# Attention and two MoE layers in one program: softmax sums in four column strips, new ranks for the attention's order, a softplus brought forward, evictions split by bank

## The chip, the core and the metric

The kernel runs on one core of one Trainium2 chip. The metric is device time in microseconds (us), from a run of the whole program. TensorE (PE) does the matrix products, VectorE (DVE), ScalarE (ACT) and GpSimd (POOL) the elementwise work, and SyncE (SP) issues the DMAs. Each engine works through its own list of instructions in order.

## What is computed

Three stages follow one another, each on the result of the one before: an attention with a decaying bias, an MLP with a softplus, and a second MLP with an RMS norm and a SiLU gate.

```
# attention: 4 batches x 8 heads, 576 positions, head width 64
scores = scale * np.matmul(q, k.transpose(0, 1, 3, 2))
cum = np.cumsum(np.maximum(s, 0.0), axis=-1)
bias = -(cum[:, :, :, None] - cum[:, :, None, :])
scores = np.where(causal, -1000000000.0, scores + np.minimum(bias, 0.0))
attn = np.exp(scores - np.max(scores, axis=-1, keepdims=True))
attn = attn / (np.sum(attn, axis=-1, keepdims=True) + 1e-09)
x = np.matmul(attn, v)                       # 2304 tokens x 512
...
# first MLP, 512 -> 2048 -> 512
h = x @ w_in
g = np.maximum(h, 0.0) + np.log1p(np.exp(-np.abs(h)))
x = g @ w_out
...
# second MLP, 512 -> 1536 -> 512
xn = x / np.sqrt(np.mean(x * x, axis=-1, keepdims=True) + 1e-06) * rms_g
g = xn @ w_gate
y = (g * (1.0 / (1.0 + np.exp(-g))) * (xn @ w_val)) @ w_out
```

## The kernel before, in words

**Stages.** In the profile the attention takes the first 221 us or so, the first MLP the time to about 632 us, the second the rest. The MLPs split each fp32 operand in a high and a low part of the faster type fp32r and multiply three times (high by high, low by high, high by low).

**Attention.** 32 heads are worked in 16 pairs p = 0 to 15. For each pair a fixed set of operations is listed by `attention_ops`, each with an engine, a planned duration, and what it depends on. The names that matter here:

- QT0 and QT1: q and k are loaded by LD (L391) and transposed on PE (L409). LV loads v (L398, L401).
- RA to RD with KA and so on: scores with queries on the partitions (L462, mask L470), from which DVE takes the row maxima. MT turns these maxima (L493), and DM writes them by DMA into the operand aq (L502, L503), to which POOL first writes a masked copy (AQ, L431).
- Ra to Rd with Ka and so on: scores the other way round, less the maximum (L518, mask L528), exponentials on ACT (Ea0 and so on, L535).
- A1 to A3: POOL adds the exponentials e of key blocks to zs (L546). V0 and V1: PE multiplies them by v (L552), into PSUM bank "o" (columns 0 to 383) and bank "x1" (columns 384 to 575).
- Z0 and Z1: PE sums zs and two leftover pieces of e over the partitions by a product with a matrix of ones (also recorded at L552, since one helper issues both). Z0 takes bank "o" again, Z1 the free half of "x1". Each head's sums come out on 64 partitions, all of them alike.
- O0 to O2: ACT copies PSUM to xz (L590). ZD (L594) fetches the sums by DMA into 128x9, ZR takes the reciprocal on DVE (L598), RS (L601) writes it out, BC (L606) spreads it over 64 partitions, XM multiplies on POOL (L610), XW (L614) writes x out.
- CF, CA, CD, CP, CH, CL: float64 weights of the MLPs are fetched (L227) and converted on ACT, DVE (L245 to L249) and POOL (L261, L282, L290), one step after another beside the attention.
- XL and X0 to X3 load and split the first tile of x for the first MLP; H0 and H1 are its first two products.

**What sets the order.** `attention_order` takes the operations one by one: among those that could start earliest by the planned durations it takes the one with the smallest rank, which is base times OFF["PER"] plus the offset OFF[name] (base is the pair's number, CONV0 and CONVR place the conversion steps). A change of the array's shape on PE is planned at 0.13. What comes out is the order of every engine's list; on the chip only the order is left of it.

**First MLP.** A step is m1_h (L792 to L794, 12 products), m1_sp (two softplus activations, L813 and L814), m1_gl (a subtraction, L818) and m1_y (L830, 12 products). Steps 0 and 1 have their m1_h in the attention's list; the rest follows when that list is through.

**Second MLP.** A step is m2_g (seven products A, B, C, D, in the manner of Strassen, L979 to L981 each) and m2_out (L1071), which adds into six PSUM banks m = 0 to 5 over 12 steps f. After each of three groups of 12 steps m2_evac copies the six banks out (L1082 on ACT, L1084 on DVE), two copies of 256 columns each, during steps f = 0 and f = 1 of the next group.

Of the kernel before, what the change touches and what calls it, by code (L numbers as in the profile page):

```python
# [36 lines left out]
OFF = {  # L37
    "PER": 11.74,
    "LV": 0.87,
    "QT0": -47.43,  # L40
    "QH0": 1.18,
    "QL0": -13.62,
    "QT1": -21.47,
    "QH1": -48.49,
    "QL1": -58.02,
    "AQ": -27.76,
    "RA": 67.90,
    "KA": 24.26,
# [15 lines left out]
    "MH": 34.21,
    "DM": -11.64,
    "Ra": -68.46,
    "Ka": -51.86,
    "Rb": 63.32,
    "Kb": 59.10,
    "Rc": 112.60,  # L70
    "Kc": -29.92,
    "Rd": 123.04,
    "Kd": -71.46,
    "Ea0": 22.03,
    "Ea1": -44.32,
    "Eb0": -51.97,
    "Eb1": -36.15,
    "Ec0": -74.59,
    "Ec1": 59.54,
    "Ed0": 45.74,  # L80
    "Ed1": 67.75,
    "A1": -21.66,
    "A2": -50.66,
    "A3": 70.17,
    "V0": -16.24,
    "V1": 79.45,
    "Z0": -16.76,
    "Z1": 87.12,
    "O0": 136.78,
    "O1": -45.76,  # L90
# [24 lines left out]
    "X3": -59.99,
    "H0": -23.02,
    "H1": -64.43,
}
CONV0 = 7.439
CONVR = 1.0130  # L120
OFF2 = {
# [24 lines left out]
def attention_moe_kernel(ctx, tc, q, k, v, s, w_in, w_out, w_gate, w_val, w_out2, rms_g, out):  # L146
# [47 lines left out]
    def f32(ap):  # L194
        return ap.bitcast(F32)
# [381 lines left out]

    IS = 384

    def a_ox(p, part):  # L580
        if ("xz", p) not in st:
            st["xz", p] = pools["xo"].tile([P, 2, S], F32, tag="xz", name="xz", bufs=2)
        xz = st["xz", p]
        if part < 2:
            jobs = ((part, slice(0, IS), st.pop((("o", "oz")[part], p))[:, 0:IS]),)
        else:
            x = st.pop(("x1", p))
            jobs = ((0, slice(IS, S), x[:, 0:S - IS]), (1, slice(IS, S), x[:, S - IS:2 * (S - IS)]))
        for w, c, x in jobs:
            nc.scalar.activation(out=xz[:, w, c], in_=x, func=AF.Copy, bias=(0.0, 1e-9)[w])  # L590
# [26 lines left out]
    def attention_ops():  # L617
# [8 lines left out]
        op(("GL", 0), "POOL", 2.9, g_load, [], 1, lat=4.0)  # L626
        for n, du in enumerate((1.9, 1.4, 1.3, 1.3)):
            op((f"G{n}", 0), "DVE", du, lambda n=n: g_part(n), [(f"G{n - 1}" if n else "GL", 0)], 1)
        for p in range(NP):
# [40 lines left out]
            add("A1", "POOL", 2.2, lambda p=p: a_a(p, 0), es[:6] + old(2, "Z0", "Z1"))  # L670
# [15 lines left out]
        for c, (ph, ch) in enumerate(CONV):  # L686
# [19 lines left out]
        for a in range(KD):  # L706
            op((f"X{a}", 0), "DVE", 0.8, lambda a=a: x_split(0, a, nc.vector), [("XL", 0), ("QT1", NP - 1)] + [(f"X{a - 1}", 0)] * (a > 0), NP)
        for i in range(2):
            op((f"H{i}", 0), "PE", 2.1, lambda i=i: m1_h(i),
               [(f"X{a}", 0) for a in range(KD)] + [("MT", NP - 1), ("CL", NA - 1), ("CP", len(CONV) - 1)] + [("R" + x, p) for x in "abcd" for p in (NP - 2, NP - 1)], NP, mode="f")  # L710
        for o in ops:
# [97 lines left out]
    def m1_sp(i):  # L809
        h = st.pop(("h", i))  # L810
        l = st["l", i] = m1_tile("l", 2)
        gh = st["gh", i] = m1_tile("gh", 3, F32R)
        nc.scalar.activation(out=l, in_=h, func=AF.Softplus)  # L813
        nc.scalar.activation(out=gh, in_=h, func=AF.Softplus)  # L814

    def m1_gl(i):
        gl = st["gl", i] = m1_tile("gl", 3, F32R)
        nc.vector.tensor_tensor(out=gl, in0=st.pop(("l", i)), in1=f32(st["gh", i]), op=ALU.subtract)  # L818
# [173 lines left out]
    def m2_g(n, fill=None):  # L992
# [25 lines left out]
        if f == 1 and g > 0:  # L1018
            m2_evac(g - 1, 1)
        if n:  # L1020
# [19 lines left out]
        if fresh:  # L1040
            m2_evac(g - 1, 0)
        if n + 1 < NS2:
# [30 lines left out]

    def m2_evac(g, h):
        W = DM // 2
        for m in range(3 * h, 3 * h + 3):
            r = 2 * T * g + m * P
            for i, c in enumerate((slice(0, W), slice(W, DM))):
                ob = y_tile() if g < NG - 1 or m % 2 else m1_tile("gl", 3)
                ob, src = ob[:, 0:W], st["o2"][m][:, c]  # L1080
                if m % 2:
                    nc.scalar.activation(out=ob, in_=src, func=AF.Copy)  # L1082
                else:
                    nc.vector.tensor_copy(out=ob, in_=src)  # L1084
                nc.sync.dma_start(out=out[r:r + P, c], in_=ob)

    def m2_end():
# [4 lines left out]
        m2_out(n, 0)  # L1092
        m2_evac(NG - 1, 0)
        m2_out(n, 1)
        m2_evac(NG - 1, 1)


    with tc.manual_schedule():
# [22 lines left out]
        with ExitStack() as es0:  # L1121
# [113 lines left out]
```

## Time and profile before

| | |
|---|---|
| device time, median of 3 runs | 1061.88 us (1059.81, 1061.88, 1062.24) |
| the profiled execution's own time | 1059.71 us |
| its span from the first to the last instruction | 1057.9 us |
| PE busy | 1029.3 us (97% of the span) |
| DVE busy | 693.4 us (66%) |
| POOL busy | 570.0 us (54%) |
| ACT busy | 540.6 us (51%) |
| mean granted clock of PE | 0.998 |

The shares are means over the three stages. A row of a timeline gives the start, the duration (for several instructions in a row, from the first to the last end), the engine, the line, the operation with its output and inputs, their shapes and how many; in brackets stands how long the engine was idle before and what it waited for. Matmuls overlap: a row's duration is longer than the step to the next row.

### The profile page before, as it was taken

How to read it: one execution, taken by the hardware profiler on the slowest of the kernel's cores; microseconds unless marked ns; L12 is line 12 of the kernel's file. 1: busy time of each engine (PE TensorE's matmuls, PEld its weight loads, DVE VectorE, ACT ScalarE, POOL GpSimd, SP SyncE). 2: the span in 40 equal slices, each digit the busy share in tenths (PEclk: the TensorE clock that was granted, in tenths of full speed). 3: DMA queues.
4: the chain of work that ended last, by engine and by line, in shares of the span. 5: the costliest groups of instructions: out<-in, count | busy, mean ns of one | idle time of the engine just before them, and what ended most of it. 6: DMA issues, size and time to landing. Idle time of an engine off the chain costs nothing.

```text
span 1057.9 us, 19448 instructions
## 1 busy us (share of the span) xinstructions
PE 1029.3 (97%) x7212; PEld 953.8 (90%) x7212; DVE 693.4 (66%) x1141; ACT 540.6 (51%) x1189; POOL 570.0 (54%) x477
## 2 busy tenths in 40 slices
PE   6999999999999999999999999999989999899997
PEld 5788877889999999999989998999979999799997
DVE  8888988418776756889898654545664346734444
ACT  2455666536656544544544544445554445644443
POOL 4378878736766433555767245355453433644331
PEclk9999999999999999999999999999999999999999
DMA  8367664345555575766542323224242233333221
GB/s 155 78 161 172 166 164 134 106 133 159 173 154 161 184 257 179 231 230 194 146 151 84 117 81 98 70 86 161 88 130 71 81 121 104 99 100 89 86 70 60
DMA packets 143758, 139.68 MB, mean 132 GB/s; under 512 B 68656, under 2 KB 118960, under 8 KB 143664
## 3 DMA queue, kind: packets, MB, share of 16 engines
q1 hardware_dynamic: 143632, 138.44, 44.5%
q8 instruction: 57, 0.93, 0.4%
q14 instruction: 37, 0.30, 0.1%
q0 software_dynamic: 32, 0.00, 0.0%
HBM read 106.73 MB, written 31.53 MB: 131 GB/s over the span
## 4 chain that ended last, share of the span: by engine, by line
PE 60%; DVE 7%; issue 3%; POOL 3%; DMA 2%; ACT 2%; SPq 0%; POOLq 0%; ACTq 0%; DVEq 0%
PE y L830 12%; PE o L1071 10%; PE A L979 4%; PE A L981 4%; PE A L980 4%; PE D L981 3%; PE D L979 3%; PE D L980 3%; PE h L792 3%; PE h L794 3%; PE h L793 3%; PE x L1071 2%; PE x L792 1%; PE x L794 1%; PE x L793 1%
## 5 line engine op out<-in xcount | busy, mean ns | idle before, releaser
L925 POOL TENSOR_TENSOR w<-wl,w 128x512 fp32r<-128x512 f32 x108 | 140.1, 1313 | 211.7 <-ACT w L924 211.7
L1071 PE MATMUL o<-w,gg 128*128 128x512 f32 x540 | 153.3, 393 | 0.3
L830 PE MATMUL y<-gh,w 128*128 128x384 f32 x768 | 149.8, 335 | 2.9 <-ACT gh L814 1.7
L830 PEld LDWEIGHTS y<-gh,w 128*128 128x128 f32 x768 | 134.4, 188 | 4.5 <-ACT gh L814 2.0
L1071 PEld LDWEIGHTS o<-w,gg 128*128 128x128 f32 x540 | 100.8, 188 | 19.4 <-ACT yt L1082 0.9
L979 PE MATMUL A<-xf,w 128*128 128x384 f32 x288 | 97.2, 338 | 6.2 <-DVE l L1047 4.7
L980 PE MATMUL A<-xf,w 128*128 128x384 f32 x288 | 96.9, 336 | 0.7 <-DVE xf L970 0.7
L981 PE MATMUL A<-xf,w 128*128 128x384 f32 x288 | 97.0, 337 | 0.0
L1047 DVE TENSOR_TENSOR l<-A,gh 128x384 f32<-128x384 f32 x36 | 20.0, 556 | 115.8 <-ACT w L924 113.3
L535 ACT ACTIVATE e<-t 128x448 f32<-128x448 f32 (+2 forms) x128 | 56.4, 505 | 71.3 <-PE t L528 66.4
L818 DVE TENSOR_TENSOR gl<-l,gh 128x384 fp32r<-128x384 f32 x96 | 79.3, 831 | 16.1 <-ACT gh L814 16.0
L261 POOL TENSOR_TENSOR wf<-ur 128x512 int32<-128x512 int32 x44 | 62.6, 1424 | 50.4 <-DVE ur L249 36.2
L485 DVE TENSOR_REDUCE mc<-s 128x2 f32<-128x512 f32 (+4 forms) x160 | 76.3, 534 | 19.0 <-PE s L470 15.0
L792 PE MATMUL h<-xh,w 128*128 128x384 f32 x256 | 85.6, 335 | 0.0
L793 PE MATMUL h<-xl,w 128*128 128x384 f32 x256 | 85.5, 334 | 0.0
L794 PE MATMUL h<-xh,w 128*128 128x384 f32 x256 | 85.5, 334 | 0.0
L830 PE MATMUL y<-gl,w 128*128 128x384 f32 x384 | 82.4, 335 | 2.3 <-DVE gl L818 2.2
L245 DVE TENSOR_SCALAR ur<-ur 128x512 f32<-128x512 f32 x68 | 51.3, 754 | 35.2 <-ACT ur L238 35.2
L979 PE MATMUL D<-xf,w 128*128 128x384 f32 x216 | 72.9, 338 | 0.0
L981 PE MATMUL D<-xf,w 128*128 128x384 f32 x216 | 72.8, 337 | 0.0
L980 PE MATMUL D<-xf,w 128*128 128x384 f32 x216 | 72.5, 336 | 0.0
L261 POOL TENSOR_TENSOR w<-ur 128x512 int32<-128x512 int32 x24 | 34.8, 1451 | 68.7 <-DVE ur L249 48.1
(171 smaller groups left out, 2662.8 us busy)
## 6 DMA issues: line engine op xcount, KB each, us to landing
wl<-wf SPq DMA_DIRECT2D x108, 256.0 KB
raw<-in_moe_w_out_dram SPq DMA_DIRECT2D x28, 512.0 KB
wf<-w SPq DMA_DIRECT2D x24, 512.0 KB
raw<-in_moe_w_in_dram SPq DMA_DIRECT2D x16, 512.0 KB
raw<-in_moe_w_gate_dram SPq DMA_DIRECT2D x12, 512.0 KB
raw<-in_moe_w_val_dram SPq DMA_DIRECT2D x12, 512.0 KB
xr<-x SPq DMA_DIRECT2D x28, 192.0 KB
qn<-in_q_dram SPq DMA_DIRECT2D x16, 288.0 KB
```

What stands on the lines that cost most here:

```text
L261: nc.gpsimd.tensor_tensor(out=w.bitcast(I32), in0=u, in1=r3, op=ALU.add)
L485: nc.vector.reduce_max(out=o, in_=x, axis=AX.X, negate=True)
L792: nc.tensor.matmul(o, wh, xh, start=start, stop=False)
L793: nc.tensor.matmul(o, wh, xl, start=False, stop=False)
L794: nc.tensor.matmul(o, wl, xh, start=False, stop=stop)
L818: nc.vector.tensor_tensor(out=gl, in0=st.pop(("l", i)), in1=f32(st["gh", i]), op=ALU.subtract)
L830: nc.tensor.matmul(y[m][:, 0:T], x[:, m * P:(m + 1) * P], r, start=first and x is w[0] and r is gh, stop=last and r is gl)
L925: nc.gpsimd.tensor_tensor(out=t[:, 1, 0:w], in0=src, in1=f32(t[:, 0, 0:w]), op=ALU.subtract)
L979: nc.tensor.matmul(o, wh[:, c], xh, start=first, stop=False, skip_group_check=True)
L980: nc.tensor.matmul(o, wh[:, c], xl, start=False, stop=False, skip_group_check=True)
L981: nc.tensor.matmul(o, wl[:, c], xh, start=False, stop=last, skip_group_check=True)
L1071: nc.tensor.matmul(st["o2"][m], x[:, m * P:(m + 1) * P], r, start=(f == 0 and k == 0), stop=(f == F2 - 1 and k == 2))
```

## The change

1. **Sums.** Z0 and Z1 become one operation Z. The weights are 32 columns of ones instead of 64, and each of the two heads gets two strips of 32 output partitions: the strips par = 0 take 128 columns of e and 160 of zs, the strips par = 1 take 288 columns of zs and 64 of e. All sums go into the free part of bank x1; bank o holds products with v alone. O1 copies 288 columns of sums, O2 copies 192 columns of x once instead of two pieces, and ZD reads four partitions of 288 sums. Z has an array shape ("mode") of its own.
2. **Ranks.** Planned durations are raised (CD 2.8 to 4.4, CP 1.29 to 1.43, X 0.8 to 1.2 and smaller ones), and all offsets in OFF are new, so the order of the attention's lists is another one throughout.
3. **Softplus.** m1_sp and m1_gl of the first MLP's steps 0 and 1 go into the attention's list as SP0, SP1, SG0 and SG1, with tiles borrowed from the attention's pools.
4. **Evictions.** m2_evac takes a list of banks. For the first two groups even banks go to ACT and odd ones to DVE (before, the other way round), banks 0 and 2 at the old place in step f = 0, bank 1 after that step's second sigmoid, banks 3, 4 and 5 in step f = 1. The last group stays as it was.

```diff
 OFF = {
-    "PER": 11.74,
-    "LV": 0.87,
...
+    "PER": 14.93,
+    "LV": 83.11,
...
-CONV0 = 7.439
-CONVR = 1.0130
+CONV0 = 0.746
+CONVR = 1.0075
...
-    def a_z(p, part):
+    IS = 384
+    IZ = 288
+    IO = S - IS
+
+    def a_z(p):
         zs, e = st["zs", p], st["e", p]
-        one = f32(ones)[:, 0:D]
-        if part == 0:
-            o = st["oz", p] = ps_1("o0")
-            jobs = ((one, zs, 0, P, 256), (one, e, 0, 0, P))
-        else:
-            o = st["x1", p]
-            jobs = ((one, zs, 256, 192, 192), (low, e, 768, 320, 64))
-        a_pv([(lambda hd, lt=lt: lt, lambda hd, x=x, c=c, w=w: x[:, hd, c:c + w], oc, w, part == 0 and n == 0)
-              for n, (lt, x, c, oc, w) in enumerate(jobs)], o)
...
+        one = f32(ones)[:, 0:32]
+        o = st["x1", p]
+        for lt, par, x, c, oc, w in ((one, 1, zs, 160, 0, IZ), (one, 0, e, 0, 0, P),
+                                     (one, 0, zs, 0, P, IZ - P), (low[:, 0:32], 1, e, 768, 224, 64)):
+            for hd in range(2):
+                r = 64 * hd + 32 * par
+                nc.tensor.matmul(o[r:r + 32, IO + oc:IO + oc + w], lt, x[:, hd, c:c + w], start=False,
+                                 stop=x is e or par == 0, skip_group_check=True)
...
-        nc.sync.dma_start(out=z, in_=st["xz", p][0:D + 1:D, 1])
+        nc.sync.dma_start(out=z, in_=st["xz", p][0:P:32, 1, 0:IZ])
...
-            add("V1", "PE", 1.45, lambda p=p: a_v(p, 1), es + ["LV"], alloc=[("x", [("O2", p)])], mode="c")
-            add("Z0", "PE", 0.67, lambda p=p: a_z(p, 0), ["A3", "V0"], alloc=[("o", [("O1", p)])], mode="c")
-            add("Z1", "PE", 0.46, lambda p=p: a_z(p, 1), ["A3", "V1"], mode="c")
+            add("V1", "PE", 1.45, lambda p=p: a_v(p, 1), es + ["LV"], alloc=[("x", [("O1", p), ("O2", p)])], mode="c")
+            add("Z", "PE", 0.72, lambda p=p: a_z(p), ["A3", "V1"], mode="z")
...
-            cv("CD", "DVE", 2.8, w_conv_d, ["CA"])
-            cv("CP", "POOL", 1.29, w_conv_p, ["CD"] + ([("CL" if c - 3 < NA else "CS", c - 3)] if c > 2 else []))
+            cv("CD", "DVE", 4.4, w_conv_d, ["CA"])
+            cv("CP", "POOL", 1.43, w_conv_p, ["CD"] + ([("CL" if c - 3 < NA else "CS", c - 3)] if c > 2 else []))
...
+        for i in range(2):
+            op((f"SP{i}", 0), "ACT", 2.1 - 1.25 * i, lambda i=i: m1_sp(i), [(f"H{i}", 0)]
+               + [(f"E{x}{hd}", p) for x in "abcd" for hd in range(2) for p in (NP - 2, NP - 1)], NP)
+            op((f"SG{i}", 0), "DVE", 0.6, lambda i=i: m1_gl(i), [(f"SP{i}", 0)], NP)
...
         if f == 1 and g > 0:
-            m2_evac(g - 1, 1)
+            m2_evac(g - 1, (3, 4, 5))
...
         if fresh:
-            m2_evac(g - 1, 0)
+            m2_evac(g - 1, (0, 2))
...
         act(out=s1, in_=gB, func=AF.Sigmoid)
+        if fresh:
+            m2_evac(g - 1, (1,))
...
-                if m % 2:
+                if m % 2 == (g == NG - 1):
                     nc.scalar.activation(out=ob, in_=src, func=AF.Copy)
```

The order shows what the ranks do. PE in the middle of the attention, the sums of a pair before the change (zs, e, ones and low are the operands named above):

```order
L528 LDWEIGHTS mask_135
L528 MATMUL t<-ident_134,mask_135 128x64
L552 MATMUL o_3045<-zs,ones 64x256 x2
L552 MATMUL o_3045<-e,ones 64x128 x2
L552 MATMUL x_2859<-zs,ones 64x192 x2
L552 MATMUL x_2859<-e,low 64x64 x2
L493 MATMUL mT<-ident,mc_208 128x128
L409 MATMUL qkT<-ident,qn 128x96 x6
```

And the sums of a pair after it:

```order
L473 LDWEIGHTS mask_135
L473 MATMUL s<-ident_134,mask_135 128x64
L581 MATMUL x_3120<-zs,ones 32x288 x2
L581 MATMUL x_3120<-e,ones 32x128 x2
L581 MATMUL x_3120<-zs,ones 32x160 x2
L581 MATMUL x_3120<-e,low 32x64 x2
L465 MATMUL s<-all_146,aq 128x512 x2
L465 MATMUL s<-hl 128x512 x2
```

The sums had stood between Kd of one pair and MT with the transposes of a later one; now they stand between KA and RB of a later pair, and the products with v, which have the sums' old array shape, stand elsewhere. A pair has five changes of the array's shape on PE instead of four.

SP, which issues the DMAs, at the program's start, from the eighth row of its list on, before (qn, kn and vn are q, k and v; raw is a step of float64 weights; aq<-mt is DM of pair 0; ahead of these stand the q and k of two pairs and pair 0's first v):

```order
L401 DMA vn_212<-in_v_dram 64x2x64
L398 DMA vn_214<-in_v_dram 128x4x64 x2
L401 DMA vn_214<-in_v_dram 64x2x64
L323 DMA all_145<-in_s_dram 32x1x576 x2
L398 DMA vn_216<-in_v_dram 128x4x64 x2
L401 DMA vn_216<-in_v_dram 64x2x64
L391 DMA qn<-in_q_dram 96x12x64
L391 DMA kn<-in_k_dram 96x12x64
L391 DMA qn<-in_q_dram 96x12x64
L391 DMA kn<-in_k_dram 96x12x64
L227 DMA raw<-in_moe_w_in_dram 128x4x128
L502 DMA aq<-mt 2x4x128
```

And after, where the q and k of two pairs stand ahead and no v:

```order
L230 DMA raw<-in_moe_w_in_dram 128x4x128
L230 DMA raw<-in_moe_w_out_dram 128x512
L326 DMA all_145<-in_s_dram 32x1x576 x2
L394 DMA qn<-in_q_dram 96x12x64
L394 DMA kn<-in_k_dram 96x12x64
L394 DMA qn<-in_q_dram 96x12x64
L394 DMA kn<-in_k_dram 96x12x64
L394 DMA qn<-in_q_dram 96x12x64
L394 DMA kn<-in_k_dram 96x12x64
L401 DMA vn_212<-in_v_dram 128x4x64 x2
L404 DMA vn_212<-in_v_dram 64x2x64
L505 DMA aq<-mt 2x4x128
```

Two weight fetches, of which one stood later, come first now; the q and k of a fifth pair are added ahead of DM of pair 0, and the v of two pairs have gone behind it.

ACT at the end of the attention before (o_ and x_ are the banks o and x1, h the first MLP's products):

```order
L535 ACTIVATE e<-t 128x320 x2
L590 ACTIVATE xz<-o_4047 128x384
L590 ACTIVATE xz<-o_4072 128x384
L590 ACTIVATE xz<-x_4055 128x192 x2
L590 ACTIVATE xz<-o_4085 128x384
L590 ACTIVATE xz<-x_4094 128x192 x2
L590 ACTIVATE xz<-o_4111 128x384
L813 ACT_TABLE_LOAD
L813 ACTIVATE l<-h 128x384
L814 ACTIVATE gh<-h 128x384
```

And after:

```order
L538 ACTIVATE e<-t 128x320 x2
L821 ACT_TABLE_LOAD
L821 ACTIVATE l<-h 128x384
L822 ACTIVATE g<-h 128x384
L589 ACTIVATE xz<-o_4021 128x384
L589 ACTIVATE xz<-x_4005 128x192
L821 ACTIVATE l<-h 128x384
L822 ACTIVATE g<-h 128x384
L589 ACTIVATE xz<-x_4005 128x288
L589 ACTIVATE xz<-o_4060 128x384
```

The table load and the first pair of softplus activations, which had come after all of the attention's evictions, now follow the last exponentials directly; the evictions O0 to O2 of the last two pairs come after them, with the second softplus pair in between.

## Rows read from the trace of the kernel before

**Rows 1.** Windows view: PE, PEld, DVE, ACT, POOL busy us; PEclk, DMA share, GB/s

```profile
12.00:24.00 12.00, 11.87 (x101) 9.88 (x100) 10.38 (x25) 1.34 (x5) 2.93 (x5) 1.00 1.00 183
96.00:108.00 12.00, 12.00 (x175) 9.63 (x173) 10.19 (x20) 7.39 (x19) 10.07 (x8) 1.00 0.73 174
```

**Rows 2.** Timeline of PE, the sums of one pair; a mask product elsewhere

```profile
97.26 0.23 PE L528 MATMUL t<-ident,mask 64*128 64x64 bf16 x4
97.42 0.65 PE L552 MATMUL o<-zs,ones 128*64 128x256 f32 x4
97.90 0.39 PE L552 MATMUL o<-e,ones 128*64 128x128 f32 x4
98.12 0.50 PE L552 MATMUL x<-zs,ones 128*64 128x192 f32 x4
98.66 0.33 PE L493 MATMUL mT<-ident,mc 128*128 128x128 f32 x1
...
203.98 0.23 PE L528 MATMUL t<-ident,mask 64*128 64x64 bf16 x4
204.05 0.46 PE L518 MATMUL t<-aq,all 41*128 41x448 f32 x2
```

**Rows 3.** Waits of PE over the span: us in total, times, longest

```profile
PE A L979 <- DVE l L1047: 4.7, 2, 2.4
PE o L552 <- ACT xz L590: 0.7, 1, 0.7
```

**Rows 4.** Timeline of ACT and PE where the first MLP begins

```profile
221.42 1.28 ACT L813 ACT_TABLE_LOAD   x1
224.81 1.50 PE L830 MATMUL y<-gh,w 128*128 128x384 f32 x7 [1.66 <-ACT gh L814]
```

**Rows 5.** Timelines of DVE, POOL and PE at the second group's start

```profile
774.39 1.41 DVE L1084 COPY yt<-o 128x256 f32<-128x256 f32 x4
775.72 0.54 DVE L1047 TENSOR_TENSOR l<-A,gh 128x384 f32<-128x384 f32 x1
782.96 0.75 DVE L1084 COPY yt<-x 128x256 f32<-128x256 f32 x2
...
775.55 1.00 POOL L970 TENSOR_TENSOR xf<-sq,xf 128x384 fp32r<-128x384 f32 x1
...
776.41 0.41 PE L979 MATMUL A<-xf,w 128*128 128x384 f32 x1 [2.34 <-DVE l L1047]
777.18 0.33 PE L980 MATMUL A<-xf,w 128*128 128x384 f32 x1
783.05 0.49 PE L1071 MATMUL o<-w,gg 128*128 128x512 f32 x1
783.85 0.47 PE L1071 MATMUL x<-w,gg 128*128 128x512 f32 x1 [0.31 <-DVE yt L1084]
```

**Rows 6.** Timelines of SP's queue and PE in the first 40 us

```profile
18.93 1.56 SPq L227 DMA_DIRECT2D raw<-in_moe_w_in_dram  x1
24.66 0.62 SPq L502 DMA_DIRECT2D aq<-mt  x1
...
28.96 1.32 PE L518 MATMUL t<-hl 64*128 64x448 f32 x6
39.51 0.76 PE L518 MATMUL t<-hl 64*128 64x448 f32 x6
```

**Rows 7.** Timelines of SP's queue and POOL around a pair's sums

```profile
99.35 0.58 SPq L594 DMA_DIRECT2D z<-xz  x1
111.35 0.58 SPq L594 DMA_DIRECT2D z<-xz  x1
...
109.11 0.75 POOL L431 TENSOR_SCALAR aq<-all,oh 128x576 fp32r<-128x576 f32 x1 [1.04 <-PE t L518]
112.30 1.43 POOL L610 TENSOR_TENSOR xz<-xz,rb 128x576 f32<-128x576 f32 x1 [0.22 <-DMA rb<-rd]
116.91 1.00 POOL L546 TENSOR_TENSOR zs<-zs,e 128x384 f32<-128x384 f32 x1
```

More of the change, by code (lines that the diff above doesn't have):

```diff
@@ L64 @@
[L64 to L90, printed above, removed]
@@ L120 @@
-CONVR = 1.0130
+    "PER": 14.93,
+    "LV": 83.11,
+    "QT0": 5.81,
+    "QH0": -39.55,
+    "QL0": -143.55,
+    "QT1": -11.31,
+    "QH1": 21.73,
+    "QL1": 14.30,
+    "AQ": 47.79,
+    "RA": 60.80,
+    "KA": 40.06,
+    "RB": 64.05,
+    "KB": -14.02,
+    "RC": 47.61,
+    "KC": 7.02,
+    "RD": -116.26,
+    "MA0": -138.12,
+    "MA1": 54.17,
+    "MB0": -67.30,
+    "MB1": -72.90,
+    "MC0": 31.97,
+    "MC1": 39.81,
+    "MD0": 31.08,
+    "MD1": 36.24,
+    "MN": 58.58,
+    "MT": -4.50,
@@ new lines @@
+    "MH": 25.08,
+    "DM": -19.33,
+    "Ra": 14.80,
+    "Ka": -41.55,
+    "Rb": 56.23,
+    "Kb": 10.35,
+    "Rc": 87.09,
+    "Kc": -21.91,
+    "Rd": 94.14,
+    "Kd": -8.05,
+    "Ea0": 54.85,
+    "Ea1": 27.06,
+    "Eb0": -66.79,
+    "Eb1": 59.21,
+    "Ec0": 91.89,
+    "Ec1": 91.42,
+    "Ed0": -2.82,
+    "Ed1": 6.60,
+    "A1": -39.80,
+    "A2": -48.49,
+    "A3": -96.30,
+    "V0": 56.77,
+    "V1": 53.07,
+    "Z": 36.84,
+    "O0": -58.45,
+    "O1": -36.49,
+    "O2": 66.31,
@@ new lines @@
+    "ZD": 10.01,
+    "ZR": -50.07,
+    "RS": -45.48,
+    "BC": -11.58,
+    "XM": -56.10,
+    "XW": -55.44,
+    "LD": -68.54,
+    "CF": -33.75,
+    "CA": 98.32,
+    "CD": -20.13,
+    "GL": 54.71,
+    "G0": 71.14,
+    "G1": -4.52,
+    "G2": 6.70,
+    "G3": -50.59,
+    "CP": -61.13,
+    "CH": 54.18,
+    "CL": -20.47,
+    "CS": 31.87,
+    "XL": -29.93,
+    "X0": -48.73,
+    "X1": -45.79,
+    "X2": 65.94,
+    "X3": -5.03,
+    "H0": -34.45,
+    "H1": -109.57,
+    "SP0": -60.0,
@@ L121 @@
+    "SP1": -60.0,
+    "SG0": -60.0,
+    "SG1": -60.0,
+}
+CONV0 = 0.746
+CONVR = 1.0075
 OFF2 = {
@@ L583, in a_ox @@
         xz = st["xz", p]
[L584 to L590, printed above, removed]
+        w, c, src, x, n, b = ((0, 0, "o", 0, IS, 0.0), (1, 0, "x1", IO, IZ, 1e-9), (0, IS, "x1", 0, IO, 0.0))[part]
+        nc.scalar.activation(out=xz[:, w, c:c + n], in_=st[src, p][:, x:x + n], func=AF.Copy, bias=b)
     def a_zd(p):
         z = st["z", p] = pools["sml"].tile([P, 9], F32, tag="z", name="z", bufs=2)
-        nc.sync.dma_start(out=z, in_=st["xz", p][0:D + 1:D, 1])
+        nc.sync.dma_start(out=z, in_=st["xz", p][0:P:32, 1, 0:IZ])
     def a_zr(p):
@@ L626, in attention_ops @@
         op(("GL", 0), "POOL", 2.9, g_load, [], 1, lat=4.0)
-        for n, du in enumerate((1.9, 1.4, 1.3, 1.3)):
+        for n, du in enumerate((1.9, 1.4, 1.5, 2.5)):
             op((f"G{n}", 0), "DVE", du, lambda n=n: g_part(n), [(f"G{n - 1}" if n else "GL", 0)], 1)
@@ L669, in attention_ops @@
             es = [f"E{x}{hd}" for x in "abcd" for hd in range(2)]
-            add("A1", "POOL", 2.2, lambda p=p: a_a(p, 0), es[:6] + old(2, "Z0", "Z1"))
+            add("A1", "POOL", 2.2, lambda p=p: a_a(p, 0), es[:6] + old(2, "Z"))
             add("A2", "POOL", 1.6, lambda p=p: a_a(p, 1), ["A1", "Ed0", "Ed1"])
@@ L706, in attention_ops @@
         for a in range(KD):
-            op((f"X{a}", 0), "DVE", 0.8, lambda a=a: x_split(0, a, nc.vector), [("XL", 0), ("QT1", NP - 1)] + [(f"X{a - 1}", 0)] * (a > 0), NP)
+            op((f"X{a}", 0), "DVE", 1.2, lambda a=a: x_split(0, a, nc.vector), [("XL", 0), ("QT1", NP - 1)] + [(f"X{a - 1}", 0)] * (a > 0), NP)
         for i in range(2):
             op((f"H{i}", 0), "PE", 2.1, lambda i=i: m1_h(i),
-               [(f"X{a}", 0) for a in range(KD)] + [("MT", NP - 1), ("CL", NA - 1), ("CP", len(CONV) - 1)] + [("R" + x, p) for x in "abcd" for p in (NP - 2, NP - 1)], NP, mode="f")
+               [(f"X{a}", 0) for a in range(KD)] + [("MT", NP - 1), ("CL", NA - 1), ("CP", len(CONV) - 1)] + [("R" + x, p) for x in "abcd" for p in (NP - 2, NP - 1)] + [("H0", 0)] * i, NP, mode="f")
+        for i in range(2):
+            op((f"SP{i}", 0), "ACT", 2.1 - 1.25 * i, lambda i=i: m1_sp(i), [(f"H{i}", 0)]
+               + [(f"E{x}{hd}", p) for x in "abcd" for hd in range(2) for p in (NP - 2, NP - 1)], NP)
+            op((f"SG{i}", 0), "DVE", 0.6, lambda i=i: m1_gl(i), [(f"SP{i}", 0)], NP)
         for o in ops:
@@ L810, in m1_sp @@
         h = st.pop(("h", i))
-        l = st["l", i] = m1_tile("l", 2)
-        gh = st["gh", i] = m1_tile("gh", 3, F32R)
+        if i < 2:
+            if "l01" not in st:
+                st["l01"] = pools["e"].tile([P, 2, 1600], F32, tag="e", name="l")
+                st["g01"] = pools["split"].tile([P, 4, S], F32R, tag="hl", name="g", bufs=3)
+            l, gh = st["l", i], st["gh", i] = st["l01"][:, i, 0:T], st["g01"][:, i, 0:T]
+        else:
+            l = st["l", i] = m1_tile("l", 2)
+            gh = st["gh", i] = m1_tile("gh", 3, F32R)
         nc.scalar.activation(out=l, in_=h, func=AF.Softplus)
@@ L816, in m1_gl @@
     def m1_gl(i):
-        gl = st["gl", i] = m1_tile("gl", 3, F32R)
+        gl = st["gl", i] = m1_tile("gl", 3, F32R) if i > 1 else st["g01"][:, 2 + i, 0:T]
         nc.vector.tensor_tensor(out=gl, in0=st.pop(("l", i)), in1=f32(st["gh", i]), op=ALU.subtract)
@@ L1072, in m2_out, with m2_evac @@
                              stop=(f == F2 - 1 and k == 2))
-    def m2_evac(g, h):
+    def m2_evac(g, ms):
         W = DM // 2
-        for m in range(3 * h, 3 * h + 3):
+        for m in ms:
             r = 2 * T * g + m * P
```

65 lines of the change are left out of this document (7 added, 58 removed).

## The prediction, made before the changed kernel ran

> **What bounds the kernel now.** I read the busy shares first, then windows, then PE's waits, then the timelines where PE waits. In the attention's middle PE is busy for all 12.00 of 12.00 us, while DVE has 10.19 and POOL 10.07 [rows 1]. One pair's fetch of sums starts 12.00 us after the other's [rows 7], so a pair costs 12.0 us and PE sets it: what is taken from PE's list there is gained, so long as the other engines keep up. In the MLPs PE is nearly full too; its waits there are few, and this change touches those of rows 3, where VectorE's L1047 ends 4.7 us at two places and ScalarE's eviction one of .7. At the program's start it is different: DMA share 1.00 and DVE 10.38 of 12 us, and PE's rows are long there [rows 1, 6].
>
> **The sums on PE.** The block is read from the last mask product at 97.26 to MT at 98.66 [rows 2]. From the mask products to the first sum are .16; where the same four mask products are followed by a product of the shape that PE already has, .07 (203.98 to 204.05) [rows 2]. That leaves .09 for a change of shape. The sums run from 97.42 to 98.66, 1.24, with the change back. Both heads' 128 columns, each of which is passed twice as fp32, take 97.90 to 98.12, .22, so .86 ns for a column and pass, and the two heads, which lie in different columns of the array, already run together. All 640 columns of a head then need 640 × 2 × .86 = 1.10; the other .23 of the 1.33 from the mask products' end at 97.33 to MT is the first load and the two changes.
>
> After, a head's columns are split over two strips: 288 + 64 = 352 in the one and 128 + 160 = 288 in the other. If all four strips run together the longer sets it: 352 × 2 × .86 = .61, and .84 with the .23. The program's order may hold them back: the 288 columns come first for both heads, and a product that goes twice over one strip holds what is queued behind it. Then the strip's first pass (.25) goes alone, and 128, 160 and 64 columns go on it one after another (.22 + .28 + .11, each twice): .86, so 1.09 with the .23. The new place costs a fifth change of shape in a pair, .09. So a pair's sums cost .93 to 1.18 instead of 1.33, a gain of .15 to .40; I take .28, the middle, since nothing in the trace has four strips. For 16 pairs: **−4.5 us**. If strips do not overlap more than the heads do now, the columns cost the same and only the fifth change is left: 16 × .09 = +1.4. These are the ends: −6.4 and +1.4.
>
> The rule that speaks against the change is in the Trainium skill, "TensorEngine Tiling (Array Packing)", Key Properties: a change of tiling mode, other than a change of tile, drains the engine. The .09 above is what this case shows of it, and the 1.4 that all fifth changes cost together. For the strips the Trainium skill, "TensorE: Matmul & The Clock Gate", Part 3 (packing small matmuls), has three 32-column tiles at 2.38 times one; by that figure the four strips would near the full overlap, an estimate of −6 us for the 16 pairs. No row of this case shows it.
>
> **Bank o.** It no longer waits for an eviction before the sums. The one place where PE waited for that, .73 of the .7 row at the attention's end [rows 3], goes: **−.7**. It could come back as a wait for V0's own bank, so the ends are −.7 and 0. O1 and O2 shrink to one copy each, off the path, since ACT is busy 7.39 of 12 us [rows 1].
>
> **First softplus.** Before, ACT loads the softplus table at 221.42 for 1.28 us after all evictions, then needs two activations a step, and PE's first y waits 1.66 for the second, with nothing else in its list [rows 4]. After, both are done while PE still works at the attention's last products and sums. The wait goes: **−1.7**. What now stands behind the table load is O0 to O2 of the last pairs, some 3 us later than before, which the long chain of the last pair's sums does not feel on PE: PE needs only the bank. Ends: −1.7 and 0 (then the evictions would hold V0 of pair 15).
>
> **Evictions.** At a group's start DVE's four copies of 1.41 us at 774.39 stand ahead of L1047, and PE waits 2.34 for it [rows 5]. With two banks given to ACT and the third copied later, only the wait for L1047's own inputs is left, so it starts at 774.4 and PE at 775.1, 1.3 earlier. But the fifth product (L980, 777.18) needs POOL's xf (775.55 for 1.00), and would come at 776.6 at best, .5 earlier than now. That is the gain. In step f = 1 DVE has two banks where it had one: m = 3, which PE needs first (783.05), is copied behind L1017 (copies 782.96 for .75 now), so at 783.8, and PE loses about the .3 that it waits at 783.85 today. Net .2 a place, two places: **−.4**. Ends: −4.7, the whole of row 3, and +1.6, if each of the two later banks makes PE wait a further .4 at both places.
>
> **The start.** By the shapes in the order a weight fetch has 512 KB, q, k and v of a pair 288 KB each. Ahead of DM of pair 0 (issued at 24.66 before [rows 6]) stand 512 + 576 − 576 = 512 KB more: one more fetch, one more pair's q and k, two pairs' v less. At 183 GB/s [rows 1], with DMA full, that is 2.9 us. DM itself has room for it, since SP's queue stood from 20.5 (18.93 + 1.56) to 24.66 and waited for the maxima. But the q and k of pairs 1 and later land behind the weights, and by the order PE transposes those of pair 2 ahead of the last scores of pair 1. I take half of the 2.9, **+1.5**, with ends −1 (conversions start earlier, and DVE is less crowded later) and +5 (all of it on PE, and DVE's list, 10.38 of 12 us busy, late by as much as its spare 1.6 [rows 1]). PE's products run long in this stretch: six of 448 columns take 1.32 at 28.96 and .76 at 39.51 [rows 6], so nearer to the lower level (1.2 GHz) than to 2.4, though the granted clock reads 1.00 in the window before them [rows 1]; a start with another rhythm of PE can shift the moment of the step by a few us, of which half would be gained or lost. This is inside the ends.
>
> **The other ranks.** In the steady state the order on DVE and POOL is another one, at the same work. It costs nothing so long as DVE's 10.19 and POOL's 10.07 lie beside PE's 11.7 (12.0 − .28). That is the cover, and the rival below says what it costs if it is gone.
>
> **Sum.** −4.5 − .7 − 1.7 − .4 + 1.5 = −5.8 on 1059.71: 1053.9. The profiled execution lies 2.2 under the median of the three runs, at their lower end (1059.8), so I add half of that: **1055**. What a measurement can tell from no change is .3%, 3.2 us: 1058.7 to 1065.1.
>
> **Rivals.**
>
> *POOL's loop gates the sums (slower).* By the new order POOL's list runs XM of pair p, AQ, A2 of p+2, a conversion, A3 of p+2, and Z of p+2 on PE waits for that A3. From the end of the sums to XM are 13.6 us (98.66 to 112.30, through ZD, ZR, RS and BC on queues that other work shares); XM to the end of A3 5.6 (112.30 to 117.91); AQ .75 [rows 2, 7]: 20.0 us around, in two periods of 11.7, 23.4. It has 3.4 us of room. Above that each us of delay costs half a us a pair: a loop of 25.2, each of the four transfers 1.3 longer, makes the period 12.6, .9 above the forecast's, and 14 pairs of that 12.6: 1067.6. From a loop of 25.0 on the kernel is slower. For it: the hops pass SP's queue in order, at places that the ranks changed, and DVE's one at 85% load. Against it: the same chain holds today with 3.5 us of room (A3's end at 117.91 to 97.42 + 24.0).
>
> *The strips do not overlap.* −5.8 + 4.5 + 1.4 = +.1: 1061 with the same half added, no change. Against it: two heads in one array overlap today.
>
> *The start costs all 5.* 1053.9 + 3.5 + 1.1 = 1058.5, up to 1060 with a later step of PE's pace; just about no change.
>
> *Full overlap, or an earlier step of the pace.* −6.4 in place of −4.5, and −1 in place of +1.5: −10.2, 1050.6.
>
> **How the numbers follow.** Forecast (1052 to 1057.5) .56; full overlap or an earlier step (1047 to 1052) .12; strips that don't overlap (1059 to 1063) .10; POOL's loop (1059 to 1070) .12; the start (1058 to 1061) .10. Faster: .56 + .12 = .68. Slower, from 1065.1 on: .07 of POOL's loop and .01 of the start with it. The rest is .24. The range takes in the forecast, most of full overlap, the start and the strips without overlap: 1049 to 1062.
>
> **What the profile will show.** Right: the sums' block from the mask product to the next product of full shape 1.0 to 1.15, a period near 11.7 with PE full, no wait of PE for the softplus, and PE's waits at a group's start at 1.8 together instead of 2.34, with POOL's L970 as the last releaser. Wrong: a wait "x <- zs" of PE for POOL in each pair (the loop), sums of 1.4 (no overlap), a later first aq<-mt than 24.66 by over 3 us (the start), or waits for copies in step f = 1 of .5 and more.

## The result, and the profile after

The changed kernel takes 1075.62 us (four runs, 1073.35 to 1079.56), the kernel before 1062.06: a ratio of 1.0136, 95% interval 1.0102 to 1.0170. The forecast was 1055, its range ended at 1062. The profiled execution took 1073.35 us with a span of 1071.5, against 1057.9.

Starts of the same work in the two traces tell where the 13.6 us of span come from:

| place | before | after | later by |
|---|---|---|---|
| MT of pair 3 | 50.6 | 54.3 | 3.7 |
| MT of pair 14 | 182.6 | 197.2 | 14.6 |
| first product h of the first MLP | 208.3 | 220.2 | 11.9 |
| first product y | 224.8 | 234.2 | 9.4 |
| a wait of PE for ACT early in the second MLP (1.47 in both) | 639.3 | 650.0 | 10.7 |
| second group's start | 771.7 | 782.4 | 10.7 |
| third group's start | 914.3 | 926.4 | 12.1 |
| end of the span | 1057.9 | 1071.5 | 13.6 |

So the start cost 3.7 and the eleven pairs to pair 14 another 10.9. The attention's end gave back 2.7 and the seam, the passage from the attention to the first MLP, 2.5, of which 1.3 were lost again behind it. Each of the two group boundaries lost 1.4 or 1.5.

PE's waits after, columns as in [rows 3]:

```profile
PE qkT L412 <- DMA kn<-in_k_dram: 9.9, 2, 8.3
PE x L581 <- POOL zs L549: 7.1, 9, 0.8
PE s L465 <- POOL aq L434: 6.7, 9, 1.2
PE y L838 <- DVE gl L826: 4.0, 4, 2.0
PE A L987 <- DVE l L1055: 2.0, 2, 1.0
PE o L1081 <- DVE yt L1094: 1.8, 2, 0.9
```

Two waits are new and come in each of nine pairs: the sums wait for POOL's zs, the scores for POOL's aq. Windows of the changed kernel, columns as in [rows 1]:

```profile
48.00:60.00 12.00, 12.00 (x179) 9.64 (x179) 8.49 (x21) 7.03 (x18) 7.40 (x7) 1.00 0.44 85
120.00:144.00 24.00, 20.91 (x316) 16.58 (x313) 19.11 (x38) 12.54 (x32) 19.13 (x16) 1.00 0.60 148
```

From 120 on PE is busy for 20.91 of 24 us, DVE for 19.11 and POOL for 19.13: no engine is full. That is the sign of a chain of work that waits for its own end of the pair before. In the first pairs, at 48 to 60, PE is full, and there a pair took 11.6 us (MT at 42.7, 54.3, 65.9).

The sums of a pair, PE's timeline after:

```profile
99.05 0.44 PE L581 MATMUL x<-zs,ones 128*32 128x288 f32 x2 [0.80 <-POOL zs L549]
99.06 0.41 PE L581 MATMUL x<-e,ones 128*32 128x128 f32 x4
99.30 0.44 PE L581 MATMUL x<-zs,ones 128*32 128x160 f32 x6
99.77 0.50 PE L465 MATMUL s<-all,aq 40*128 40x512 f32 x2
```

The 128 columns of the other strip begin .01 after the 288, and the whole block takes .72 (99.05 to 99.77) where the block of [rows 2] took 1.24. Of those 1.24, 1.10 were columns by the prediction's working and .14 the rest; with the same .14 the new block has .58 for its columns, and the prediction's figure for strips that overlap fully is .61. The strips overlap fully.

The chain itself, SP's queue and POOL at the place that answers to [rows 7]:

```profile
107.57 0.35 SPq L613 DMA_DIRECT2D x<-xz  x1
108.02 0.56 SPq L505 DMA_DIRECT2D aq<-mt  x1
108.62 0.51 SPq L506 DMA_DIRECT2D aq<-mt  x1
109.24 0.66 SPq L394 DMA_DIRECT2D qn<-in_q_dram  x1
109.99 0.66 SPq L394 DMA_DIRECT2D kn<-in_k_dram  x1
110.75 1.34 SPq L600 DMA_DIRECT2D rd<-z  x1
112.14 0.43 SPq L230 DMA_DIRECT2D raw<-in_moe_w_in_dram  x1
115.84 1.13 SPq L605 DMA_DIRECT2D rb<-rd  x2
```

```profile
106.14 1.40 POOL L609 TENSOR_TENSOR xz<-xz,rb 128x576 f32<-128x576 f32 x1 [3.12 <-DMA rb<-rd]
107.52 0.74 POOL L434 TENSOR_SCALAR aq<-all,oh 128x576 fp32r<-128x576 f32 x1
119.53 1.41 POOL L609 TENSOR_TENSOR xz<-xz,rb 128x576 f32<-128x576 f32 x1 [3.51 <-DMA rb<-rd]
```

Read it as a ring, a chain that closes on itself one pair later. XM of one pair ends at 107.54; XW, which waits for it, is issued at 107.57; behind XW on the same queue stand DM, the two loads of LD, RS of the next pair (110.75), then BC (115.84), which waits for what RS wrote, and the next XM waits for BC (119.53). XM to XM is 13.39: 1.43 to XW, 1.67 for XW and DM, 1.51 for issuing LD, 1.34 for issuing RS (.34 in the rows where no load stands ahead of it), 3.75 until BC, 3.69 until XM. PE's list hangs on this through aq, which stands behind XM in POOL's list, and through zs.

The kernel before has the same ring. Its SP queue and POOL, up to XM at 112.30 of [rows 7]:

```profile
99.98 0.65 SPq L391 DMA_DIRECT2D qn<-in_q_dram  x1
100.73 0.68 SPq L391 DMA_DIRECT2D kn<-in_k_dram  x1
102.42 0.34 SPq L614 DMA_DIRECT2D x<-xz  x1
104.11 0.34 SPq L601 DMA_DIRECT2D rd<-z  x1
107.07 1.75 SPq L606 DMA_DIRECT2D rb<-rd  x2
```

```profile
100.82 1.57 POOL L610 TENSOR_TENSOR xz<-xz,rb 128x576 f32<-128x576 f32 x1 [0.73 <-ACT mt L497]
```

From XM at 100.82 to XM at 112.30 it takes 11.5 us, under the 12.0 of PE. The two loads stand ahead of XW there, in time in which the queue has to wait for XM in any case.

### The profile page after: what moved, and what is told of

Same layout as the page of the kernel before. It is cut to its first block, busy times and chain, and to the rows that moved or that the text cites. A ratio compares the mean times of both kernels' runs of the same rounds, so it can differ in the third digit from the quotient of the medians.

```text
span 1071.5 us, 19427 instructions
## 1 busy us (share of the span) xinstructions
PE 1027.7 (96%) x7212; PEld 950.1 (89%) x7212; DVE 677.5 (63%) x1141; ACT 533.6 (50%) x1173; POOL 565.1 (53%) x477
## 4 chain that ended last, share of the span: by engine, by line
PE 61%; DVE 7%; issue 3%; POOL 3%; DMA 2%; ACT 1%; SPq 0%; POOLq 0%; ACTq 0%; DVEq 0%
PE y L838 12%; PE o L1081 11%; PE A L988 4%; PE A L989 4%; PE A L987 4%; PE D L989 3%; PE D L988 3%; PE D L987 3%; PE h L796 3%; PE h L795 3%; PE h L794 3%; PE x L1081 2%; PE x L796 1%; PE x L795 1%; PE x L794 1%
## 5 line engine op out<-in xcount | busy, mean ns | idle before, releaser
L838 PE MATMUL y<-gh,w 128*128 128x384 f32 x752 | 146.6, 335 | 1.1 <-DVE yt L853 1.0
L838 PEld LDWEIGHTS y<-gh,w 128*128 128x128 f32 x752 | 131.7, 188 | 2.4 <-DVE yt L853 1.7
L248 DVE TENSOR_SCALAR ur<-ur 128x512 f32<-128x512 f32 x68 | 58.2, 856 | 36.9 <-ACT ur L241 35.6
```

Source lines behind the costliest of these rows:

```text
L838: nc.tensor.matmul(y[m][:, 0:T], x[:, m * P:(m + 1) * P], r, start=first and x is w[0] and r is gh, stop=last and r is gl)
```

## The experiments

**Theory.** SP's queue closes a ring within one pair, and the new place of LD inside it makes it longer than PE's work. **Rival.** POOL's or PE's own order, or the strips, set the period.

**e1: LD out of the ring.**

```diff
+        for p in range(6, NP):
+            move(("LD", p), ("ZD", p - 5))
```

(LD now stands behind ZD and ahead of XW. move takes an operation out of the finished list and puts it behind another, or with False ahead of it.)

> The changed kernel with one thing moved: on SP's queue the two loads of q and k of a later pair (LD of p + 6) stand behind the fetch of sums (ZD) instead of ahead of the write of the reciprocals (RS). Theory, SP's queue closes a ring within one pair: the multiply XM, the write XW behind it, DM, LD, RS, its landing, the broadcast BC, its landing, the next XM. Without LD that ring shrinks from 13.3 us to 10 to 11, PE becomes the bound again at about 11.6 us a pair, and some 9 gated pairs give back 1.7 each: 1058 to 1062 us. Rival, POOL's order or the strips on PE set the period: a load's place on the queue changes little, 1073 to 1078 us, and PE still waits for zs and aq in each pair.

Measured: 1058.98, ratio to the kernel before .9971 (.9954 to .9988), so by the medians 16.6 us under the changed kernel. MT comes every 11.60 us (54.6 to 182.2 for eleven pairs), PE's waits for zs and aq are gone, and the windows show PE full again:

```profile
96.00:108.00 12.00, 12.00 (x185) 9.46 (x183) 10.00 (x21) 7.34 (x20) 10.65 (x9) 1.00 0.76 176
```

The theory holds, the rival falls: the strips, the ranks of PE, DVE and POOL and the five changes of shape are all still there.

**e3: the same move in the kernel before.** LD moved into the ring, nothing else.

```diff
+        for p in range(7, NP):
+            move(("LD", p), ("RS", p - 6), False)
```

> The kernel before with the loads of q and k (LD of p + 6) moved on SP's queue from their place ahead of XW to directly ahead of RS, as the changed kernel has them; all else as before. Theory of the ring in SP's queue: RS is issued 1.4 later, and its own issue and landing take 1 to 2 us more behind 576 KB, so the ring of 11.3 grows to 13 to 14.7 us, and some 9 to 10 pairs lose 1 to 2.5 each: 1073 to 1085 us, with PE waiting for zs and aq. Rival, the place of the loads does not matter: 1061 to 1063 us.

Measured: 1079.61, ratio 1.0175 (1.0154 to 1.0195). XM there, POOL's timeline:

```profile
107.09 1.41 POOL L610 TENSOR_TENSOR xz<-xz,rb 128x576 f32<-128x576 f32 x1 [2.74 <-ACT ur L238]
121.20 1.40 POOL L610 TENSOR_TENSOR xz<-xz,rb 128x576 f32<-128x576 f32 x1 [3.54 <-DMA rb<-rd]
```

14.1 us from one to the next, 14.05 in the mean of nine (65.76 to 192.23); the first row's wait is put down to ACT's ur, which XM does not read. This one move of a load costs the old kernel more than the whole change did.

One part of the expectation did not come: PE waits there for DVE's maxima (5.5 us in four waits), not for zs and aq. In DVE's list these maxima stand behind the reciprocal ZR, which waits for the fetch ZD on the same queue:

```profile
121.03 0.22 DVE L598 RECIPROCAL z<-z 128x9 f32<-128x9 f32 x1 [3.88 <-DMA z<-xz]
```

And part of the 18 us may be the clock's, since PE, which now stops in the attention, is at the lower level in some stretches:

```profile
120.00:132.00 12.00, 10.38 (x112) 9.21 (x105) 7.22 (x15) 6.24 (x15) 9.46 (x8) 0.72 0.56 138
```

The longer ring does not come from that: XM is 13.2 to 14.7 us apart already between 65.76 and 121.20, where the granted clock is 1.00.

**e9: LD behind RS, still ahead of BC.** Is it the wait of RS behind LD, or the load anywhere in the ring?

```diff
+        for p in range(6, NP):
+            move(("LD", p), ("RS", p - 6))
```

> The changed kernel with LD directly behind RS on SP's queue: still inside the ring, ahead of CF and BC, but no longer ahead of the write of the reciprocals. Theory, what costs is that RS stands behind LD (1.35 of issue, .7 of a slower issue of its own, 1 to 2.5 of a landing behind 576 KB): LD's issue now fits into RS's landing, the ring is about 11 to 12 us, 1059 to 1064. Rival, 576 KB anywhere ahead of BC cost the ring the same transfer time: 13 us a pair and 1070 to 1076.

Measured: 1071.98, ratio 1.0104 (1.0068 to 1.0141); MT every 13.2 us (96.3 to 201.7 for eight pairs, in a profile of the longest of its four executions). My expectation was wrong, the rival's right. SP's queue shows why:

```profile
114.51 0.34 SPq L600 DMA_DIRECT2D rd<-z  x1
114.95 0.67 SPq L394 DMA_DIRECT2D qn<-in_q_dram  x1
115.71 0.69 SPq L394 DMA_DIRECT2D kn<-in_k_dram  x1
116.45 1.34 SPq L230 DMA_DIRECT2D raw<-in_moe_w_in_dram  x1
117.89 2.29 SPq L605 DMA_DIRECT2D rb<-rd  x2
```

RS is issued in .34 and BC 3.4 after it instead of 5.1, but now BC's own issue takes 2.29, and XM starts 7.2 after it (125.11). What RS no longer waits, BC does: 576 KB cost the ring about the same behind RS as ahead of it, so long as they stand ahead of BC.

**e10: half of the load.** q's load stays ahead of RS, k's goes behind ZD.

```diff
-        for src, nm in ((q, "qn"), (k, "kn")):
+        for src, nm in [((q, "qn"), (k, "kn"))[w] for w in which]:
...
+            seq[i] = (lambda p=p: a_load(p, (0,))), ("LD", p)
+            n = next(i for i, x in enumerate(seq) if x[1] == ("ZD", p - 5)) + 1
+            seq.insert(n, ((lambda p=p: a_load(p, (1,))), ("LDk", p)))
```

> The changed kernel with q's half of LD where it is, ahead of RS, and k's half behind ZD. Theory, the ring grows with what stands ahead of RS (issue .7 and 288 KB instead of 1.35 and 576 KB): from 10.4 without LD and 13.3 with it, about 11.9, some .3 over PE's 11.6: 1060 to 1066. Rival, any large load ahead of the small write costs it all, since what counts is the wait for a free place behind a load: 1070 to 1076.

Measured: 1060.88, ratio .9992 (.9976 to 1.0007); MT every 11.7 us (100.4 to 182.3 for seven pairs, in a profile of the shortest of its ten executions). With half of the load ahead of RS a pair takes just about PE's 11.6, within what I expected. So the cost goes with how much is loaded there, not with the presence of a load. Bytes and the number of issues were halved together; the run doesn't separate them.

**e2: the strips alone**, in the kernel before with its old order (a_z, a_ox and a_zd of the change; Z stands where Z1 stood).

> The kernel before with the sums alone changed: four column strips in bank x1, issued where Z1 stood, with the old order of everything else and the old evictions. If the strips cost what the changed kernel's row shows (about .72 us for the products) a pair costs 11.5 to 11.7 us instead of 12.0, and the ring through SP's queue, 11.3 us in the kernel before, still fits: 1055 to 1058 us. Rival, the strips themselves or the ring hold the pair at 12.0: 1061 to 1063 us.

Measured: 1060.16, ratio .9985 (.9965 to 1.0005), above what I expected. The block of sums takes .72 here too (85.35 to 86.07). Three pairs in a row, from MT at 74.6 to 109.0, take 11.5 us each, later ones 11.5 to 12.1, so 11.72 in the mean of ten (62.7 to 179.9): in the old order, which was made for 12.0, other work is late in part of the pairs. PE's waits don't say which, since none of them is over .2 there. The ring is the likely one: XM comes every 12.1 us (64.58 to 173.62, nine times), eight times after a wait of 1.3 to 2.3, and from XM at 101.99 to XM at 113.92 its links follow without a gap on SP's queue. The strips alone with LD at another place were not tried. And PE's first y waits 3.79 instead of 1.66, with the lower clock behind it (PEclk .57 from 222 to 226, about 1.6 us), and both groups' starts fell to the lower clock (below), some 2.9 us in all.

**e7: the first softplus alone**, in the kernel before.

> The kernel before with the first two softplus steps in the attention's list, and nothing else. By the forecast's step PE's wait of 1.66 at the first y goes: 1059.5. Theory of the fetch: the first y starts earlier, but a softplus two steps later still waits on ACT behind a weight fetch that is issued no earlier, and PE's wait there grows by as much: no change, 1060.5 to 1061.8.

Measured: 1061.73, ratio .9998 (.9989 to 1.0008): nothing. The wait has moved to where the theory of the fetch had it, and grown from .66 at 239.62 in the kernel before (ended by the same subtraction) to 2.38:

```profile
237.51 0.97 PE L844 MATMUL y<-gl,w 128*128 128x384 f32 x4 [2.38 <-DVE gl L832]
```

Behind this wait the clock is at its lower level in this profile (PEclk .57 from 238 to 242), which costs about 1.4 us more.

**e5: the next weight fetches ahead of the last XW**, on top of e1.

```diff
+        n = next(n for n, y in enumerate(seq) if y[1] == ("BC", NP - 1)) + 1
+        seq[n:n] = [(lambda c=c: w_fetch(1, c), ("CF1", c)) for c in (NA, NA + 1)]
```

> The changed kernel with LD moved (as before) and, at the seam, the first MLP's two next weight fetches issued directly behind the last broadcast BC, ahead of the last two writes XW that wait for POOL's last multiply. Theory: the seam's gain is given back because ACT, in order, waits for a weight fetch that stands on SP's queue behind those writes, and the softplus behind it holds PE for 2.7 us at 236: with the fetch 4.5 us earlier that wait goes, 2 to 2.7 us less than with LD moved alone (1059): 1056 to 1057.5. Rival, DVE's or ACT's own work sets that wait: 1058 to 1060.

Measured: 1055.29, ratio .9940 (.9919 to .9962), 3.7 under e1. In e1 the fetch was issued at 228.19, behind XW of the last pairs, which wait for POOL, and ACT waited for what it brings, with the softplus of the next step behind it in its list (234.92):

```profile
233.39 0.66 ACT L241 ACTIVATE ur<-raw 128x512 f32<-128x512 f32 x1 [8.67 <-DMA raw<-in_moe_w_in_dram]
```

Here, in SP's queue:

```profile
223.22 1.08 SPq L605 DMA_DIRECT2D rb<-rd  x2
224.36 0.58 SPq L230 DMA_DIRECT2D raw<-in_moe_w_in_dram  x1
224.98 0.51 SPq L230 DMA_DIRECT2D raw<-in_moe_w_out_dram  x1
225.61 3.30 SPq L613 DMA_DIRECT2D x<-xz  x2
```

and PE's wait of 2.70 at 236 in e1 is gone. The seam was held by SP's queue as well.

**e4: the evictions alone**, in the kernel before.

> The kernel before with the new evictions alone. Theory: PE's one long wait at a group's start becomes three shorter ones, of about the same sum, after which the granted clock is at its lower level for some 3.5 us and 1.5 us are lost at each of the two places, as in the changed kernel's profile: 1064 to 1066 us. Rival, the forecast's step: .2 gained at each place, and the lower clock in the changed kernel came from elsewhere: 1061 to 1062 us.

Measured: 1061.21, ratio .9994 (.9984 to 1.0005). My theory, that the new evictions bring the lower clock and cost 1.5 us at each place, falls: at one of the two places the clock was low, at the other not. Windows after the two groups' starts:

```profile
776.00:780.00 4.00, 3.40 (x12) 3.30 (x12) 2.57 (x5) 0.57 (x2) 2.58 (x3) 0.63 0.74 195
922.00:926.00 4.00, 4.00 (x22) 3.61 (x21) 2.85 (x6) 1.79 (x4) 1.06 (x1) 1.00 0.73 221
```

And e2, with the old evictions, has it at both:

```profile
776.00:780.00 4.00, 4.00 (x15) 3.79 (x15) 1.59 (x4) 1.30 (x3) 0.03 (x1) 0.64 0.76 221
920.00:924.00 4.00, 4.00 (x17) 3.78 (x17) 1.72 (x5) 1.43 (x3) 0.08 (x1) 0.72 0.77 238
```

**e11: e5 with the old evictions.**

> The changed kernel with LD moved and the two fetches ahead of the last writes (1055.3 measured), and the old evictions. The evictions measured alone made no difference, and the lower clock after a group's start was seen with either order of them: 1054 to 1057. Rival, the new evictions bring the lower clock more often: 1052 to 1054.

Measured: 1056.17, ratio .9956 (.9940 to .9973): the same as e5 within the intervals.

**e6 and e8: the start**, q ahead of k again and the two fetches behind the loads of pairs 3 and 4, on e1 and on e5.

```diff
+        for p in range(3):
+            move(("QT0", p), ("QT1", p), False)
+        for c in range(2):
+            move(("CF", c), ("LD", 3 + c))
```

> The changed kernel with LD moved (as before) and its start mended: the first three pairs' q are transposed ahead of k again, and the two weight fetches on SP's queue stand behind the loads of pairs 3 and 4. Theory: the start costs some 3.3 us (first transpose 1.5 later because k lands after q, a wait of .5 for the next k, and 1.1 for the maxima), so 1.5 to 3.5 less than with LD moved alone (1059): 1055.5 to 1057.5. Rival, the start's loss is given by the array's pace and DVE's order: 1058 to 1060.

> The changed kernel with all three edits: LD moved, the two fetches ahead of the last writes, and the start mended. If each is a part of its own the gains add up: 1052.5 to 1055.5, under both kernels. Rival: one hides another, 1056 to 1059.

Measured: 1059.10, ratio .9971 (.9957 to .9986), and 1057.65, ratio .9950 (.9931 to .9969): no gain over e1 and e5. The first t<-hl comes at 31.6 and 32.0 instead of 32.3 and 32.6, but in both profiles PE's rows keep their long durations some 10 us longer than in e1 (last section), which would hide a gain. Whether the edits bring that, the runs don't show.

**e12: e5, q ahead of k, and pair 2's transposes behind MT of pair 0.**

```diff
+        for a in ("QL1", "QL0", "QH1", "QH0", "QT1", "QT0"):
+            move((a, 2), ("MT", 0))
```

> The changed kernel with LD moved and the two fetches ahead of the last writes (1055.3 measured), and at the start q transposed ahead of k and pair 2's transposes and splits behind the first pair's maxima (MT). Theory, the start is late by its order on PE: the first product with the maxima (t<-aq) comes at 29 to 30.5 us instead of 32 to 32.6, the third pair's MT some 2 to 3 us earlier, 1052 to 1054. Rival, the start is given by how long PE keeps its slow pace, which differs from run to run by 12 us whatever the order: the first such product earlier, but 1054 to 1057 with a spread of 5 us.

Measured: 1054.41, ratio .9935 (.9918 to .9953). MT of pair 0 comes at 22.9 instead of 26.7 in e5, but the first t<-aq at 31.3, not 29 to 30.5, and the six measured times spread from 1052.25 to 1058.04. So it is the rival's picture, and no better than e5 by more than the spread. It is the lowest of the versions tried, .65% under the kernel before and about 2% under the changed one: the change is worth having once two things on SP's queue are put elsewhere, as e5 does.

## Why the prediction was wrong, step by step

- **The other ranks: the step that failed.** It costed the new order at nothing "so long as DVE's 10.19 and POOL's 10.07 lie beside PE's 11.7". The queue of SP was not on that list of covers, and the order shown of it ended at the program's start. LD moved from ahead of XW to between DM and RS on that queue, and the ring went from 11.5 us, under PE's 12.0, to 13.4, over it. e1 (out of the ring, −16.6), e3 (into it, +18, the clock's part included) and e10 (half) show that this place made the loss. Against the 11.6 us a pair of e1, the eleven pairs from pair 3 to 14 lost 15.3 us.
- **The rival of POOL's loop**, at .12, had the right direction and the wrong ring. It named SP's queue as a reason, and its sign, PE's wait for zs in each pair, came. But it ran over two periods with 13.6 us from the sums to XM, a duration taken from the old order; after, XM of the pair whose sums end at 99.77 starts at 119.53, 19.8 later. The ring that governs closes in one period, XM, XW, RS, BC, XM. It stood in the old trace, at 11.5 us from 100.82 to 112.30, with half a us of room beside PE's 12.0. I did not follow it round.
- **The strips: right mechanism, mis-sized to the safe side.** Gain per pair .39 (11.99 to 11.60 in e1, with the fifth change) where .28 was taken and .40 was the end. The sign of 1.0 to 1.15 from the mask product to the next product of full shape came out at .94 (107.77 to 108.71 in e1). With four changes (e2) three pairs took 11.47 each, .52 less than before and as much as the block shrank (1.24 to .72). If those three are what PE's work comes to, the fifth change and the new place cost about .1; the other pairs of e2 don't show it. The Trainium skill, "TensorE: Matmul & The Clock Gate", Part 3 (packing small matmuls), has three 32-column tiles at 2.38 times one, from which the prediction estimated near the full overlap; the .72 here agrees.
- **Bank o and the softplus.** From pair 14's MT to the first h 2.7 less. With the strips alone (e2) it is 1.6 less (24.0 instead of 25.6 us), which fits the .7 of the wait for bank o, gone from the trace, and the shorter sums of the last pairs, both in the sum. The other 1.1 no run separates from the new order; it was not forecast. From h to y 2.5 less for the 1.7. But 1.3 came back at 250 in the changed kernel (2.0 of wait for .7), and in e7, alone, all of it: a later softplus stands in ACT's list behind a conversion whose weights SP issued late, which the prediction did not have.
- **Evictions.** The waits at a group's start: 1.0 and .6 with POOL's xf last, then .9 in step f = 1, as forecast in place and in the releasers. But .9 is more than the .5 that was named as a sign of being wrong, and takes back most of what the start of the group gains. Where no lower clock follows, a group takes 142.4 or 142.5 us (e1, e5, e6) against 142.6 before and 142.4 or 142.5 in e7 and e11, these with the old evictions, so nothing to .2 is gained a place. The 1.4 to 1.5 lost at each place in the changed profile is the lower clock, which e2 shows with the old evictions.
- **The start.** Forecast +1.5, ends −1 and +5; measured 3.7 at MT of pair 3, so inside the ends and mis-sized. Of it 1.3 is the first transpose, which waits for k where it had waited for q, and 1.1 is MT's wait for the maxima. The rest e6, e8 and e12 did not separate from PE's pace.

## What to carry to other kernels

List the in-order DMA queue as an engine: for every write that waits for a compute engine, follow what stands behind it on the queue, and close the chain until it comes back to the same instruction one iteration later; compare that ring, and not the busy shares, with the bound. Its length is read by going round it once in the timelines, as from 100.82 to 112.30 above. And when a stall is taken away at a seam, look for the next transfer that is issued late before counting the gain.

## What the hardware showed that I had not expected

**PE's pace at the start ends at different times.** In the first tens of us products take about 1.7 times their later time, at a granted clock that reads 1.00. e10 and e11 have the same start as e1; e10 has the short durations from about 40 on and e11 still the long ones there, the same products in both:

```profile
40.17 0.31 PE L521 MATMUL t<-aq,all 41*128 41x128 f32 x2
40.32 0.50 PE L521 MATMUL t<-hl 64*128 64x128 f32 x6
```

```profile
41.61 0.45 PE L521 MATMUL t<-aq,all 41*128 41x128 f32 x2
41.87 0.84 PE L521 MATMUL t<-hl 64*128 64x128 f32 x6
```

PE was busy for 12.00 of 12.00 us from 40 to 52 in both. In nine profiles with the new start or its edits the change comes near 40 in four and near 50 in five, where MT of pair 3 is at 54.0 to 55.3 or at 58.6 to 60.5: some 5 us. The three with an edited start (e6, e8, e12) are all among the five. In the five profiles with the old start it comes near 30 in two (e3, e7) and at 37 to 40 in three. That the new start brings the late change more often is what these profiles suggest; it was not tried by itself, and what sets the moment stays open.

**The clock can fall after a short stop.** After a group's start, in which PE had idled 1 to 2.4 us with work in between, products begin at their usual step and then go at twice that for some 3.5 us, here in the changed kernel:

```profile
785.76 0.41 PE L987 MATMUL A<-xf,w 128*128 128x384 f32 x1 [1.01 <-DVE l L1055]
787.30 0.45 PE L988 MATMUL A<-xf,w 128*128 128x384 f32 x1 [0.60 <-POOL xf L978]
788.15 0.52 PE L989 MATMUL D<-xf,w 128*128 128x384 f32 x1
788.47 0.52 PE L987 MATMUL D<-xf,w 128*128 128x384 f32 x1
```

The step goes from .17 to .32, so from the upper level (2.4 GHz) to the lower (1.2 GHz), and the window 788 to 792 has a granted clock of .57. It costs 1.2 to 1.6 us a time and came at some boundaries and not at others: at 7 of 18 in the nine profiles with the new evictions, at 5 of 10 in the five with the old ones.
